# One kernel, one change: w_out made float32 during attention, kept in DRAM, and split in two parts at MoE 1

## The chip, the cores and the metric

The kernel runs on one core of one Trainium2 chip. The metric is the device time of one execution in microseconds. Five engines take part: PE (TensorE; its weight loads are listed as PEld), DVE (VectorE), ACT (ScalarE), POOL (GpSimd) and SP (SyncE, which only issues DMAs here). Each engine works through its own instructions in a fixed order and waits on semaphores for the others.

## The reference, cut to what matters

Three stages follow each other: attention with a position bias, a first MoE block (MoE 1, one dense "expert" with a SoLU and a layer norm), and a routed MoE with eight experts of which each token takes two. MoE 1 is the stage that reads `w_out`:

```
h    = x @ w_in                                # x 1152 x 512, w_in 512 x 1024
e    = exp(h - max(h));  sm = e / (sum(e) + 1e-9)
solu = h * sm
ln   = (solu - mean) / sqrt(var + 1e-6) * g_ln
out  = ln @ w_out                              # w_out 1024 x 512
```

`w_in` and `w_out` are float64 in DRAM. [...]

## The kernel before, in words

**Bias and attention.** The position bias is made in 18 pieces (`mix`, lines 192 to 210): eight threshold masks a piece (`masks`, line 179, spread over DVE, ACT and POOL by the MASK_ENG strings; 128 x 576 each), then matmuls (L202), then two DVE operations (L207, L208) into a tile that SP writes to DRAM (`biasd`, L210). Six pieces are made ahead of attention. Attention (loop at line 375) takes 40 units (5 row blocks x 4 head pairs x 2 batches) in 40 steps k, plus a tail. A step k holds, in this order: the transposes of unit k-2 (`tr`, L329 and L331, copied out by ACT at L332 and L334), at even k the product with v (`av`, L352, L361, then ACT L364 and DVE L365), the scores of unit k (`qk`: L301 on PE, L310 on DVE adds the bias and takes the row extreme, L317 on ACT is the exponential), and, for k below 24, half a bias piece (`bias_step`). Scores, bias matmuls and transposes share three PSUM banks named `d`; a matmul that writes a `d` bank waits until the reader of the bank three allocations earlier is done.

**The conversion.** `f64_parts` (line 244) turns a chunk of 128 x 512 float64 into float32 and its two parts in seven operations: ACT L251 (absolute value of the high word), a maximum (L252), DVE L254 (shift and mask), DVE L255 and L256 (`scalar_tensor_tensor`, which bring in the sign and the low word), ACT L257 (high part `hi`) and a subtraction L258 on POOL (low part `lo`). The first five work in a tile `t64`, of which there are TB = 2; the raw words lie in a tile `raw64`, of which there are RB64 = 3. L258 is the last to read a chunk's `t64`.

**w_in** (8 chunks) is converted inside the attention loop: from step 20 on a new chunk every second step (`CONV`), and each step runs one operation of every chunk in work. Every one of these is held by `keep_in_program_order`, so that it is issued behind everything that was written down before it for its engine. **w_out** (8 chunks) is fetched at the end of attention and converted in MoE 1 (`conv_out`, lines 429 to 434, called at lines 685 and 686 behind `stage1(1)`), all seven operations of a chunk one after the other; the maximum is on POOL for the first four chunks and on DVE for the rest. These are not held, so the scheduler places them by readiness.

**MoE 1** runs nine tiles of 128 tokens: `stage1` (line 439: split of x at L442 and L443, 24 matmuls L448 into one of two PSUM banks `ps`, then DVE L453, ACT L454, DVE L455 to L457, ACT L459, DVE L460; L457 is the last reader of the bank), `stage2a` (8 transposes L479, split at L401 and L402), `stage2` (24 matmuls L487 with the two parts of w_out) and `stage3` (L499, L504). `stage2(t)` stands in the code behind `stage1(t + 2)` and `stage2a(t + 1)`.

Of the kernel before, what the change touches and what calls it, by code (L numbers as in the profile page):

```python
# [9 lines left out]
F32 = mybir.dt.float32  # L10
F32R = mybir.dt.float32r
# [4 lines left out]
AF = mybir.ActivationFunctionType  # L16
OP = mybir.AluOpType
# [8 lines left out]
DM, FF, E = 512, 1024, 8  # L26
JB = 5
CAP = 320
W2B = 10
TB = 2  # L30
RB64 = 3
EB = 8
LAG = 2
# [7 lines left out]
AB = 1  # L41
SF = 3
TK = {0: (0, 1), 1: (2, 3)}
CONV = (20, 22, 24, 26, 28, 30, 32, 34)
TR = 7
FM = 2

# [16 lines left out]
def build(tc, I, O):  # L64
    nc = tc.nc
    ctx = ExitStack()
    with ctx:
        _build(tc, nc, ctx, I, O)


def _build(tc, nc, ctx, I, O):
    consts = ctx.enter_context(tc.tile_pool(name="consts", bufs=1, reuse_waits="tile"))

    dram = ctx.enter_context(tc.tile_pool(name="dram", bufs=1, space=bass.MemoryType.DRAM))
    x1d = dram.tile([NT * 128, DM], F32, name="x1d")
    biasd = dram.tile([NG, 128, S], F32, name="biasd")
    out = O["out"]

    nc.scalar.preload_act_table_set("natural_log_exp_and_others")
# [4 lines left out]
    V, P_ = nc.vector, nc.gpsimd  # L84
# [3 lines left out]
    def pool(stack, name, **kw):  # L88
        return stack.enter_context(tc.tile_pool(name=name, bufs=1, **{"reuse_waits": "tile", **kw}))
# [5 lines left out]
    cv = pool(ph_, "cv", side="right")  # L95
# [20 lines left out]
    def load_q(it):  # L116
        Q[it] = kvp.tile([128, 8, 128], F32, name="q", bufs=2)
        nc.sync.dma_start(Q[it], I["q5"][it])
# [27 lines left out]
    with tc.high_priority():  # L146
# [4 lines left out]
        for a in range(2):  # L151
            P_.tensor_tensor(out=W[:, a], in0=wab[:, a, None, :].to_broadcast([128, 4, H]),
                             in1=bd[:, 0:4, None].to_broadcast([128, 4, H]), op=OP.mult)
# [58 lines left out]
    def bias_step(s):  # L212

        m, gg = divmod(s, 2)
        if m >= NM:
            return
        if m + 1 < NM:
            masks(m + 1, 4 * gg, 4 * gg + 4)
        mix(m, gg)
# [3 lines left out]
    def bias_in(n):  # L223

        it, hp = divmod(n, 4)
        if it > 4:
            return
        r = 8 if it < 4 else 4
        src = biasd[8 * it:8 * it + r].rearrange("g (q h) j -> (g q) h j", h=H)[:, 2 * hp:2 * hp + 2]
        t = BT[it, hp] = btp.tile([128, 2, S], F32, name="bt", bufs=6)  # L230
        if it < 4:
            nc.sync.dma_start(t, src)
        else:
            for x in range(2):
                nc.sync.dma_start(t[64 * x:64 * x + 64, 0], src[:, x])


    def fetch(src):

        raw = cv.tile([128, 1024], F32, name="raw64", bufs=RB64)  # L240
        nc.sync.dma_start(raw.bitcast(mybir.dt.int64), src)
        return raw

    def f64_parts(raw, hi, lo, eng, eng2, pin=lambda i: i):

        tf = cv.tile([128, 512], F32, name="t64", bufs=TB)
        r = raw.bitcast(U32).rearrange("p (n two) -> p n two", two=2)
        w0, w1 = r[:, :, 0], r[:, :, 1]
        tu = tf.bitcast(U32)

        return (lambda: pin(nc.scalar.activation(tf, w1.bitcast(F32), AF.Abs)),  # L251
                lambda: pin(eng.tensor_scalar(tf, tf, 2.0 ** -15, None, op0=OP.max)),  # L252

                lambda: pin(V.tensor_scalar(tu, tu, 3, 0x3FFFFFF8, op0=OP.logical_shift_left, op1=OP.bitwise_and)),  # L254
                lambda: pin(V.scalar_tensor_tensor(tu, w1, 0xC0000000, tu, op0=OP.bitwise_and, op1=OP.bitwise_or)),  # L255
                lambda: pin(V.scalar_tensor_tensor(tu, w0, 29, tu, op0=OP.logical_shift_right, op1=OP.bitwise_or)),  # L256
                lambda: pin(nc.scalar.activation(hi, tf, AF.Copy)),  # L257
                lambda: pin(eng2.tensor_tensor(out=lo, in0=tf, in1=hi.bitcast(F32), op=OP.subtract)))  # L258

    CI = (V, P_)  # L260
    CO = [(P_, P_)] * 4 + [(V, P_)] * 4
    WI = {}

    def fetch_in(k, a):
        return fetch(I["w_in"][k * 128:k * 128 + 128, a * 512:a * 512 + 512])

    def conv_in(k, a, raw):

        if a == 0:
            if k < 3:  # L270
                t = bp.tile([128, 2304], F32R, name="mk", bufs=3)
                t = [t[:, 0:1024], t[:, 1024:2048]]
            else:
                t = [bp.tile([128, 1152], F32R, name="t", bufs=3) for w in range(2)]
            for n in range(2):
                WI[k, n] = [t[w][:, n * 512:n * 512 + 512] for w in range(2)]
        return f64_parts(raw, *WI[k, a], *CI, tc.keep_in_program_order)


    A = [(it, hp, b) for it in range(5) for hp in range(4) for b in range(B)]  # L280
# [39 lines left out]
    def tr(it, hp, b):  # L320

        u, es = SU[it, hp], ES.pop((it, hp, b))
        n = len(es)
        if b == 0:
            u.rest = psum.tile([128, 4, 128], F32, name="rest")
        pt = dbank().rearrange("p x (j i) -> p x j i", j=4)
        for x, e in enumerate(es):
            for jb in range(4):
                nc.tensor.transpose(pt[:, x, jb], e[:, jb * 128:jb * 128 + 128], ident)  # L329
        for x, e in enumerate(es):  # L330
            nc.tensor.transpose(u.rest[:, n * b + x], e[:, S - 128:S], ident)  # L331
        nc.scalar.activation(u.et[:, n * b:n * b + n, 0:4], pt[:, 0:n], AF.Copy)  # L332
        if b == 1:
            nc.scalar.activation(u.et[:, 0:2 * n, 4], u.rest[:, 0:2 * n], AF.Copy)  # L334
            u.rs = ap.tile([128, 4], F32, name="rs", bufs=3)
            V.tensor_scalar(u.rs[:, 0:2 * n], u.sums[:, 0:2 * n], 1e-9, None, op0=OP.add)
            V.reciprocal(u.rs[:, 0:2 * n], u.rs[:, 0:2 * n])
            if n == 2:
                u.rb = ap.tile([128, 4, 64], F32, name="rb", bufs=2)
                P_.tensor_copy(u.rb, u.rs[:, :, None].to_broadcast([128, 4, 64]))  # L340
# [29 lines left out]
    tc.keep_in_program_order(nc.scalar.preload_act_table_set("natural_log_exp_and_others"))  # L370
    bias_in(0)
    bias_in(1)
    chunks = [(k, a) for k in range(4) for a in range(2)]
    raws, conv = [], []
    for k in range(len(A) + LAG + 8):
        if k % 2 == 0 and k < len(A):
            bias_in(k // 2 + 2)
        if k % 8 == 6 and k // 8 + 1 < 5:
            load_q(k // 8 + 1)
        if LAG <= k < len(A) + LAG:  # L380
            tr(*A[k - LAG])
        if LAG <= k - 1 < len(A) + LAG and A[k - 1 - LAG][2] == 1:
            av(*A[k - 1 - LAG][:2])
        if k < len(A):
            qk(*A[k])
        bias_step(2 * PRE + k)
        if k == CONV[0] - 6:
            raws = [fetch_in(*chunks.pop(0)) for c in range(RB64)]
        if k in CONV:
            n = CONV.index(k)  # L390
            conv.append(list(conv_in(n // 2, n % 2, raws.pop(0))))
        for fs in conv:
            if fs:
                fs.pop(0)()
                if len(fs) == 2 and chunks:
                    raws.append(fetch_in(*chunks.pop(0)))
    pa.close()


# [16 lines left out]
    wop = pool(ph_, "wop", side="right")  # L416
    pm_ = ctx.enter_context(ExitStack())
    mp = pool(pm_, "mp", side="right")
    WO = {}

    def fetch_out(f):
        return fetch(I["w_out"][f * 128:f * 128 + 128, :])

    raws = [fetch_out(f) for f in range(RB64)]
    gB = mp.tile([128, FF], F32, name="gB")
    junk = mp.tile([128, FF], BF, name="junk")
    nc.sync.dma_start(gB, I["g_ln"].to_broadcast([128, FF]))

    def conv_out(f):
        WO[f] = [wop.tile([128, 512], F32R, name=f"wo{f}{w}") for w in range(2)]  # L430
        for g in f64_parts(raws.pop(0), *WO[f], *CO[f]):
            g()
        if f + RB64 < 8:
            raws.append(fetch_out(f + RB64))

    PASSES = ((0, 0), (0, 1), (1, 0))
    ST, SO = {}, {}
# [85 lines left out]
    def rt(shape, name, dt=F32, **kw):  # L523
        return mp.tile(shape, dt, name=name, **kw)
# [158 lines left out]
    nc.sync.dma_start(gw, I["gw"])  # L683
    stage1(1)
    for f in range(8):
        conv_out(f)
    noise = rt([128, NT, E], "noise")
    nc.sync.dma_start(noise, I["noise"])
    nc.sync.dma_start(cst, I["c_p"])
# [1 line left out]
    nc.sync.dma_start(iof, I["c_iota"].to_broadcast([128, NJ * 128]))  # L691
    trif = rt([128, 128], "trif")
    nc.sync.dma_start(trif, I["c_tri"])
    zero = mp.tile([128, DM // 2], F32, name="zero")
    tc.keep_in_program_order(nc.gpsimd.memset(zero, 0.0))
    for d in (0, DM // 2):
        nc.gpsimd.dma_start(out.rearrange("(t p) d -> p t d", p=128)[:, :, d:d + DM // 2],
# [98 lines left out]
    for e in range(E):  # L796
        W2 = [wload(w2s(e, f), ep, W2B, held=True) for f in range(4)] if e else []
        xt, w1 = XG.pop(e), W1.pop(e)
        for f in range(8):
            ph = psum.tile([128, 512], F32, name="phe", tag="h", bufs=3)  # L800
            for k in range(4):
                for n, (ww_, wx) in enumerate(PAS):
# [4 lines left out]
                                   op0=OP.max, op1=OP.subtract)  # L807
# [125 lines left out]
```

## Time and profile before

| | |
|---|---|
| median of 3 runs | 639.88 us (639.5 to 641.44) |
| the profiled execution | 640.86 us, its span 639.1 us |
| mean granted TensorE clock | 0.98 |
| busy in the span | PE 91%, PEld 74%, DVE 61%, ACT 53%, POOL 36% |
| chain that ended last | PE 65%, DVE 8%, POOL 7%, issue 7%, ACT 5%, DMA 4% |
| HBM | 67.66 MB read, 20.84 MB written |

The span is what the profiler saw; 1.8 us lie around it. Bias pieces ahead of attention fill the first 45 us or so, attention runs to about 230 us, MoE 1 from there to about 360 us, and the routed MoE to the end. A busy share is a mean over these stages. The chain of work that ended last is followed back from the last instruction, at each step to what released it.

### The profile page before, as it was taken

How to read it: one execution, taken by the hardware profiler on the slowest of the kernel's cores; microseconds unless marked ns; L12 is line 12 of the kernel's file. 1: busy time of each engine (PE TensorE's matmuls, PEld its weight loads, DVE VectorE, ACT ScalarE, POOL GpSimd, SP SyncE). 2: the span in 40 equal slices, each digit the busy share in tenths (PEclk: the TensorE clock that was granted, in tenths of full speed). 3: DMA queues.
4: the chain of work that ended last, by engine and by line, in shares of the span. 5: the costliest groups of instructions: out<-in, count | busy, mean ns of one | idle time of the engine just before them, and what ended most of it. 6: DMA issues, size and time to landing. Idle time of an engine off the chain costs nothing.

```text
span 639.1 us, 12762 instructions
## 1 busy us (share of the span) xinstructions
PE 581.8 (91%) x5068; PEld 475.4 (74%) x5068; DVE 392.2 (61%) x909; ACT 341.1 (53%) x657; POOL 231.9 (36%) x177
## 2 busy tenths in 40 slices
PE   0878999999999976999999989999999999999990
PEld 0556777777767754788888788888898989898980
DVE  4987777766665659765546788774647474543400
ACT  6935656565677645554436436554545454544410
POOL 4999998960111365410000302222222222222111
PEclk9979999999999997999999999999999999999996
DMA  8694415315421242140313235756565666636212
GB/s 318 263 340 140 156 75 186 110 48 214 161 85 67 71 149 98 40 158 18 125 53 92 96 119 170 249 144 212 163 199 182 182 194 162 222 66 191 35 18 29
DMA packets 33943, 89.44 MB, mean 140 GB/s; under 512 B 3600, under 2 KB 5136, under 8 KB 33872
## 3 DMA queue, kind: packets, MB, share of 16 engines
q1 hardware_dynamic: 26480, 72.04, 31.3%
q0 software_dynamic: 5808, 13.37, 10.5%
q10 hardware_dynamic: 1584, 3.11, 1.4%
q8 instruction: 42, 0.69, 0.4%
q14 instruction: 29, 0.24, 0.1%
HBM read 67.66 MB, written 20.84 MB: 138 GB/s over the span
## 4 chain that ended last, share of the span: by engine, by line
PE 65%; DVE 8%; POOL 7%; issue 7%; ACT 5%; DMA 4%; SPq 0%; POOLq 0%; DVEq 0%
PE phe L803 16%; PE poe L786 11%; PE ps L448 6%; PE d L301 4%; PE poe L790 4%; PE av L487 4%; POOL mk L190 4%; PE av L361 4%; PE d L202 3%; PE d L329 3%; DMA out<-y,si 3%; PE pt L487 3%; ACT e L317 2%; PE pg L674 1%; PE pt L504 1%
## 5 line engine op out<-in xcount | busy, mean ns | idle before, releaser
L190 POOL TENSOR_SCALAR mk<-T,thr 128x576 bf16<-128x576 f16 x67 | 116.1, 1746 | 12.7 <-PE d L202 8.7
L803 PE MATMUL phe<-xgt,wp 128*128 128x320 f32 x768 | 115.9, 310 | 2.3 <-ACT xgt L401 2.3
L803 PEld LDWEIGHTS phe<-xgt,wp 128*128 128x128 f32 x768 | 113.2, 188 | 3.0 <-ACT xgt L401 2.5
L637 POOL DMA_INDIRECT out<-y,si x24 | 39.4, 1642 | 149.2 <-ACT y L793 73.5
L786 PE MATMUL poe<-wp,hT 128*128 128x512 f32 x384 | 90.9, 393 | 0.0
L786 PEld LDWEIGHTS poe<-wp,hT 128*128 128x128 f32 x384 | 71.0, 188 | 14.2
L317 ACT ACTIVATE e<-e,nm 128x576 f32<-128x576 f32 x72 | 55.3, 769 | 42.4 <-DVE nm L310 42.4
L202 PE MATMUL d<-mk,wd 128*32 128x288 bf16 x1152 | 49.1, 304 | 21.8 <-POOL wd L169 14.3
L806 DVE SCALAR_TENSOR_TENSOR hT<-phe,hT 128x320 fp32r<-128x320 f32 x64 | 31.3, 490 | 50.2 <-ACT hT L805 49.7
L202 PEld LDWEIGHTS <-wd 128*32 128x32 f16 x1152 | 30.2, 101 | 42.5 <-issue 18.4
L310 DVE CUSTOM_DVE_ANT_0 e<-d,bt 128x576 f32<-128x576 f32 x72 | 51.9, 755 | 15.0 <-PE d L301 15.0
L448 PE MATMUL ps<-mk,xs 128*128 128x512 f32 x162 | 43.4, 418 | 8.3 <-DVE so L457 5.7
L402 DVE TENSOR_TENSOR wp<-w2raw,wp 128x1024 fp32r<-128x1024 f32 x32 | 39.1, 1225 | 18.4 <-ACT wp L401 16.7
L301 PE MATMUL d<-kv,q 64*128 64x288 f32 x256 | 48.9, 439 | 1.6 <-DVE t L208 1.3
L805 ACT ACTIVATE hT<-phe 128x320 fp32r<-128x320 f32 x64 | 28.0, 437 | 41.3 <-PE phe L803 41.3
L361 PE MATMUL av<-et,kv 128*64 128x128 f32 (+1 forms) x800 | 45.4, 265 | 0.0
L448 PEld LDWEIGHTS ps<-mk,xs 128*128 128x128 f32 x162 | 32.1, 201 | 16.9 <-ACT xs L442 7.1
L329 PE MATMUL d<-ident,e 128*128 128x128 f32 x288 | 40.5, 282 | 4.5 <-ACT et L332 2.6
L665 POOL DMA_INDIRECT xg<-x1d,gi x21 | 21.7, 1032 | 62.0 <-DVE si L627 46.0
L329 PEld LDWEIGHTS d<-ident,e 128*128 128x128 f32 x288 | 31.6, 142 | 16.7 <-DVE nm L310 6.9
L361 PEld LDWEIGHTS av<-et,kv 128*64 128x64 f32 x800 | 40.3, 137 | 3.6 <-issue 3.2
L332 ACT ACTIVATE et<-d 128x1024 f32<-128x1024 f32 (+1 forms) x40 | 37.2, 931 | 6.9 <-PE d L329 6.7
(194 smaller groups left out, 968.5 us busy)
## 6 DMA issues: line engine op xcount, KB each, us to landing
wraw<-moe_w SPq DMA_DIRECT2D x32, 512.0 KB, 5.3
w2raw<-moe_w SPq DMA_DIRECT2D x32, 512.0 KB, 6.5
biasd<-t SPq DMA_DIRECT2D x18, 576.0 KB, 3.4
bt<-biasd SPq DMA_DIRECT2D x16, 576.0 KB, 6.4
kv<-kv SPq DMA_DIRECT2D x8, 608.0 KB, 10.1
raw<-w_in SPq DMA_DIRECT2D x8, 512.0 KB, 5.1
raw<-w_out SPq DMA_DIRECT2D x8, 512.0 KB, 3.3
q<-q SPq DMA_DIRECT2D x5, 512.0 KB, 3.5
```

Source lines behind the costliest of these rows:

```text
L190: (V if e == "D" else P_).tensor_scalar(dst, w, thr[:, 0, q:q + 1], None, op0=OP.is_gt)
L202: nc.tensor.matmul(ps[32 * u:32 * u + 32, half, 0:288], WD[n][:, 32 * a:32 * a + 32], mk[:, 4 * gg + u, half * 288:half * 288 + 288], star ...
L301: nc.tensor.matmul(ss[x][:, a, 0:288], Q[it][h, n], k[h, a * 288:a * 288 + 288], start=True, stop=True)
L310: V.tensor_tensor_reduce(out=e.rearrange("p (a b) -> p a b", a=2), in0=ps[:, :, 0:288], in1=BT[it, hp][:, x].rearrange("p (a b) -> p a b", ...
L317: nc.scalar.activation(e, e, AF.Exp, bias=nm, scale=-1.0, accum_out=u.sums[:, c + x:c + x + 1])
L329: nc.tensor.transpose(pt[:, x, jb], e[:, jb * 128:jb * 128 + 128], ident)
L361: nc.tensor.matmul(o[64 * x:64 * x + 64, 0, b, 0:n], v[:, jb, 64 * x:64 * x + 64], w, start=(jb == 0), stop=(jb == JB - 1))
L448: nc.tensor.matmul(ph[:, a], xs[wx][:, k], WI[k, a][ww], start=(k == 0 and n == 0), stop=(k == 3 and n == 2))
L487: nc.tensor.matmul(po, lt[wx][:, f], WO[f][ww], start=(f == 0 and n == 0), stop=(f == 7 and n == 2))
L637: nc.gpsimd.indirect_dma_start(out=dst, out_offset=bass.IndirectOffsetOnAxis(ap=si, axis=0), in_=y, in_offset=None, compute_op=OP.add, bou ...
L786: nc.tensor.matmul(po, hT[f][wh][:, j:j + R], W2[f // 2][ww_][:, c:c + N], start=(f == 0 and m == 0), stop=(f == 7 and m == 2))
L803: nc.tensor.matmul(ph[:, 0:CAP], w1[k][ww_][:, f * 128:f * 128 + 128], xt[wx][:, k], start=(k == 0 and n == 0), stop=(k == 3 and n == 2))
```

## The change

`f64_parts` is split. `f32` holds the first five operations (the maximum always on DVE). The parts are two operations more, ACT and POOL. The attention loop now converts 16 chunks: the eight of w_out from step 4 on and the eight of w_in from step 20 on as before, again one operation a step and chunk. A chunk of w_out ends with a DMA on SP's queue that writes the float32 tile to a DRAM buffer `w32d`. At MoE 1, `parts_out` reads a chunk back into a `t64` tile and makes the two parts. TB goes from 2 to 3, the raw fetches are now held in program order (the first three at step 1), and the zeros for the output are written from a `t64` tile instead of a tile of their own.

```diff
-TB = 2
+TB = 3
-CONV = (20, 22, 24, 26, 28, 30, 32, 34)
+CONV = (4, 6, 8, 10, 12, 14, 16, 18, 20, 22, 24, 26, 28, 30, 32, 34)
...
+    w32d = dram.tile([8, 128, 512], F32, name="w32d")
...
+    def words(c):
...
+        raw = cv.tile([128, 1024], F32, name="raw64", bufs=RB64)
+        tc.keep_in_program_order(nc.sync.dma_start(raw.bitcast(mybir.dt.int64), src))
...
+    def conv_out(c, raw):
+        t = t64()
+        return f32(raw, t) + [lambda: tc.keep_in_program_order(nc.sync.dma_start(w32d[c], t))]
...
-        if k == CONV[0] - 6:
-            raws = [fetch_in(*chunks.pop(0)) for c in range(RB64)]
+        if k == CONV[0] - 3:
+            raws = [words(chunks.pop(0)) for c in range(RB64)]
         if k in CONV:
             n = CONV.index(k)
-            conv.append(list(conv_in(n // 2, n % 2, raws.pop(0))))
+            conv.append([5] + (conv_out(n, raws.pop(0)) if n < 8 else conv_in(*divmod(n - 8, 2), raws.pop(0))))
...
-    raws = [fetch_out(f) for f in range(RB64)]
...
-    def conv_out(f):
-        WO[f] = [wop.tile([128, 512], F32R, name=f"wo{f}{w}") for w in range(2)]
-        for g in f64_parts(raws.pop(0), *WO[f], *CO[f]):
-            g()
-        if f + RB64 < 8:
-            raws.append(fetch_out(f + RB64))
+    def parts_out(f):
+        hi, lo = WO[f] = [wop.tile([128, 512], F32R, name=f"wo{f}{w}") for w in range(2)]
+        t = t64()
+        nc.sync.dma_start(t, w32d[f])
+        nc.scalar.activation(hi, t, AF.Copy)
+        P_.tensor_tensor(out=lo, in0=t, in1=hi.bitcast(F32), op=OP.subtract)
...
     for f in range(8):
-        conv_out(f)
+        parts_out(f)
...
-    zero = mp.tile([128, DM // 2], F32, name="zero")
+    zero = t64()[:, 0:DM // 2]
```

## Rows read from the trace of the kernel before

**Rows 1.** Windows: start and end, length, busy PE, PEld, DVE, ACT, POOL, clock, DMA
```profile
78.20:88.80 10.60, 10.34 (x144) 7.83 (x143) 7.84 (x19) 6.20 (x14) 9.02 (x7) 1.00 0.26 97
232.00:264.00 32.00, 24.69 (x101) 19.41 (x102) 25.99 (x46) 15.90 (x31) 17.46 (x13) 0.89 0.22 74
```

**Rows 2.** Chain of waits in MoE 1: start, length, engine, line, count
```profile
286.23 2.10 PE av L487 x9
...
293.17 5.60 PE ps L448 x24
298.77 0.87 PE pt L479 x8
299.64 2.10 PE pt L487 x9
```

**Rows 3.** Timeline, MoE 1's front: start, length, engine, work, idle before it and releaser
```profile
230.38 1.19 PE L448 MATMUL ps<-mk,xs 128*128 128x512 f32 x4 [0.89 <-ACT xs L442]
...
233.25 3.54 PE L448 MATMUL ps<-mk,xs 128*128 128x512 f32 x14 [1.68 <-DVE xs L443]
...
248.06 1.27 DVE L457 SCALAR_TENSOR_TENSOR so<-ps,st,so 128x1024 f32<-128x1024 f32 x1
...
249.49 7.20 PE L448 MATMUL ps<-mk,xs 128*128 128x512 f32 x18 [5.70 <-DVE so L457]
```

**Rows 4.** Groups of the conversion's operations: busy us, mean ns, idle before and releasers
```profile
L251 ACT ACTIVATE t<-raw 128x512 f32<-128x512 f32 x16 | 10.7, 670 | 11.4 <-POOL mk L258 5.4 <-POOL wo L258 4.8 <-POOL t L258 1.2
L252 DVE TENSOR_SCALAR t<-t 128x512 f32<-128x512 f32 x12 | 5.4, 451 | 13.4 <-ACT t L251 13.4
L254 DVE TENSOR_SCALAR t<-t 128x512 uint32<-128x512 uint32 x16 | 9.4, 590 | 8.0 <-POOL t L252 8.0
L255 DVE SCALAR_TENSOR_TENSOR t<-raw,t 128x512 uint32<-128x512 uint32 x16 | 11.0, 685 | 0.1
L256 DVE SCALAR_TENSOR_TENSOR t<-raw,t 128x512 uint32<-128x512 uint32 x16 | 12.1, 756 | 0.1
```

**Rows 5.** Timeline of two attention steps that still hold bias work
```profile
81.74 0.42 DVE L365 TENSOR_TENSOR XA<-XA,av 128x256 f32<-128x256 f32 x1 [1.41 <-ACT XA L364]
...
85.11 1.02 ACT L332 ACTIVATE et<-d 128x1024 f32<-128x1024 f32 x1 [0.20 <-PE d L329]
...
86.50 0.76 DVE L310 CUSTOM_DVE_ANT_0 e<-d,bt 128x576 f32<-128x576 f32 x1 [0.93 <-PE d L301]
...
87.99 0.86 PEld L329 LDWEIGHTS d<-ident,e 128*128 128x128 f32 x8 [0.31 <-DVE nm L310]
```

**Rows 6.** Timeline: DVE operations that ran beside POOL operations
```profile
77.59 6.96 POOL L190 TENSOR_SCALAR mk<-T,thr 128x576 bf16<-128x576 f16 x4 [0.79 <-PE d L202]
...
233.12 1.77 DVE L256 SCALAR_TENSOR_TENSOR t<-raw,t 128x512 uint32<-128x512 uint32 x1
...
236.89 2.94 POOL L252 TENSOR_SCALAR t<-t 128x512 f32<-128x512 f32 x2
...
238.41 0.83 DVE L254 TENSOR_SCALAR t<-t 128x512 uint32<-128x512 uint32 x1 [3.52 <-POOL t L252]
```

**Rows 7.** Timeline of attention after the last bias piece, and of its end
```profile
163.50 2.40 PE L361 MATMUL av<-et,kv 128*64 128x128 f32 x40
...
171.95 2.40 PE L361 MATMUL av<-et,kv 128*64 128x128 f32 x40
...
174.75 0.67 ACT L251 ACTIVATE t<-raw 128x512 f32<-128x512 f32 x1 [0.89 <-POOL mk L258]
...
180.97 2.40 PE L361 MATMUL av<-et,kv 128*64 128x128 f32 x40
...
224.17 0.43 DVE L254 TENSOR_SCALAR t<-t 128x512 uint32<-128x512 uint32 x1 [1.78 <-POOL t L252]
```

**Rows 8.** DMA issues: tile, queue, count, KB each, median us to landing
```profile
biasd<-t SPq DMA_DIRECT2D x18, 576.0 KB, 3.4
...
raw<-w_out SPq DMA_DIRECT2D x8, 512.0 KB, 3.3
```

More of the change, by code (lines that the diff above doesn't have):

```diff
@@ L235, in bias_in, with f32 @@
                 nc.sync.dma_start(t[64 * x:64 * x + 64, 0], src[:, x])
[L238 to L246, printed above, removed]
+    def f32(raw, tf):
+        pin = tc.keep_in_program_order
         r = raw.bitcast(U32).rearrange("p (n two) -> p n two", two=2)
@@ L249, in f64_parts, with t64 @@
         tu = tf.bitcast(U32)
-        return (lambda: pin(nc.scalar.activation(tf, w1.bitcast(F32), AF.Abs)),
-                lambda: pin(eng.tensor_scalar(tf, tf, 2.0 ** -15, None, op0=OP.max)),
+        return [lambda: pin(nc.scalar.activation(tf, w1.bitcast(F32), AF.Abs)),
+                lambda: pin(V.tensor_scalar(tf, tf, 2.0 ** -15, None, op0=OP.max)),
                 lambda: pin(V.tensor_scalar(tu, tu, 3, 0x3FFFFFF8, op0=OP.logical_shift_left, op1=OP.bitwise_and)),
                 lambda: pin(V.scalar_tensor_tensor(tu, w1, 0xC0000000, tu, op0=OP.bitwise_and, op1=OP.bitwise_or)),
[L256 to L261, printed above, removed]
+                lambda: pin(V.scalar_tensor_tensor(tu, w0, 29, tu, op0=OP.logical_shift_right, op1=OP.bitwise_or))]
+    def t64():
+        return cv.tile([128, 512], F32, name="t64", bufs=TB)
+    def words(c):
+        k, a = divmod(c - 8, 2)
+        src = I["w_out"][c * 128:c * 128 + 128, :] if c < 8 else I["w_in"][k * 128:k * 128 + 128, a * 512:a * 512 + 512]
+        raw = cv.tile([128, 1024], F32, name="raw64", bufs=RB64)
+        tc.keep_in_program_order(nc.sync.dma_start(raw.bitcast(mybir.dt.int64), src))
+        return raw
     WI = {}
-    def fetch_in(k, a):
-        return fetch(I["w_in"][k * 128:k * 128 + 128, a * 512:a * 512 + 512])
+    def conv_out(c, raw):
+        t = t64()
+        return f32(raw, t) + [lambda: tc.keep_in_program_order(nc.sync.dma_start(w32d[c], t))]
     def conv_in(k, a, raw):
@@ L276, in conv_in @@
                 WI[k, n] = [t[w][:, n * 512:n * 512 + 512] for w in range(2)]
-        return f64_parts(raw, *WI[k, a], *CI, tc.keep_in_program_order)
+        t, (hi, lo), pin = t64(), WI[k, a], tc.keep_in_program_order
+        return f32(raw, t) + [lambda: pin(nc.scalar.activation(hi, t, AF.Copy)),
+                              lambda: pin(P_.tensor_tensor(out=lo, in0=t, in1=hi.bitcast(F32), op=OP.subtract))]
     A = [(it, hp, b) for it in range(5) for hp in range(4) for b in range(B)]
@@ L372, in _build @@
     bias_in(1)
-    chunks = [(k, a) for k in range(4) for a in range(2)]
+    chunks = list(range(16))
     raws, conv = [], []
@@ L386, in _build @@
         bias_step(2 * PRE + k)
-        if k == CONV[0] - 6:
-            raws = [fetch_in(*chunks.pop(0)) for c in range(RB64)]
+        if k == CONV[0] - 3:
+            raws = [words(chunks.pop(0)) for c in range(RB64)]
         if k in CONV:
             n = CONV.index(k)
-            conv.append(list(conv_in(n // 2, n % 2, raws.pop(0))))
+            conv.append([5] + (conv_out(n, raws.pop(0)) if n < 8 else conv_in(*divmod(n - 8, 2), raws.pop(0))))
         for fs in conv:
[L393 to L396, printed above, removed]
+            if len(fs) > 1:
+                fs.pop(1)()
+                fs[0] -= 1
+                if fs[0] == 0 and chunks:
+                    raws.append(words(chunks.pop(0)))
     pa.close()
@@ L419, in _build @@
     WO = {}
-    def fetch_out(f):
-        return fetch(I["w_out"][f * 128:f * 128 + 128, :])
-    raws = [fetch_out(f) for f in range(RB64)]
     gB = mp.tile([128, FF], F32, name="gB")
```

## The prediction, made blind

> **What bounds the kernel now.** I read the windows first, stage by stage, since the busy shares of the whole span mix stages. In attention with bias work, two steps take 10.6 us and PE is busy for 10.34 of them; DVE for 7.84, ACT for 6.20, POOL for 9.02 [rows 1]. So PE ends these steps, with little room on DVE and POOL. In the front of MoE 1 it is the reverse: of 32 us PE is busy for 24.69 and DVE for 25.99, and the granted clock falls to 0.89 on average [rows 1]. The chain of waits then shows MoE 1 in its steady state, where one tile takes 299.64 - 286.23 = 13.41 us and all pieces are PE's [rows 2]. The timeline of the front says why it is slower: the first matmuls stop for 1.68 us because the DVE split of x is late, and the third tile's matmuls wait 5.70 us for L457, the last reader of their bank, which DVE reaches only at 248.06 because the conversion of w_out stands in the same queue. [...]
>
> **What goes: conversion work in MoE 1's front.** Per chunk one ACT operation (0.67), the maximum, L254, L255 and L256: for eight chunks 8 x (0.45 + 0.59 + 0.69 + 0.76) = 20 us of DVE at the groups' means (four maxima were on POOL, so 18) and 5.4 us of ACT [rows 4]. The price on the path is taken from PE, not from this sum. From the first L448 (230.38) to the start of the third tile's stage2 (286.23) pass 55.85 us [rows 2, 3]. At full clock PE has there five stage1 (5 x 5.60), four stage2a (4 x 0.87) and two tiles of stage2 with stage3 (13.41 - 5.60 - 0.87 = 6.94 each): 28.0 + 3.5 + 13.9 = 45.4 us [rows 2]. So 10.4 us at most can come back. Not all will: the first transposes need the whole chain of the first tile (L453 to L460), about 1.4 us behind the end of the second tile's stage1 if PE keeps the order of the code, and some 0.5 us go to the first split of x. I take 8.5, between 3 (ACT or the reloads late instead, below) and 10.4. What stays per chunk, one ACT copy and one POOL subtraction, is off the path as long as the eighth chunk is ready by the first stage2, some 18 us after the start (three stage1 and two stage2a). The reload of 256 KB should land no later than the 512 KB fetch did (3.3) [rows 8], and three `t64` tiles are in rotation, so I count under 2 us a chunk: ready after about 16.
>
> **What goes: the wait for `t64`.** With two tiles the ACT operation of a chunk waits for the POOL subtraction of the chunk two before (5.4 us in all for POOL mk, 0.89 of it at 174.75), and what ACT does next, the copy of the scores' product, is late with it [rows 4, 7]. Two steps without that wait took 171.95 - 163.50 = 8.45 us, the next two with it 180.97 - 171.95 = 9.02 [rows 7]. With three tiles the chunk before last is long done. I take 0.5 us for each of four pairs after the bias, 0.4 for each of the four short pairs of the last row block, and at the end, where DVE stood 1.78 us behind POOL's maximum of a w_out chunk [rows 7], 0.5 of that: together 4.0 us, bounds 1 and 6.
>
> **What is added: w_out's five operations beside the bias.** About eight pairs of steps (k = 4 to 23, less the ramp at both ends) get one chunk each: on ACT 0.67 (on top of 6.20 of 10.6, in idle time), on DVE two `tensor_scalar` and two `scalar_tensor_tensor`, 0.42 + 0.42 + 0.69 + 0.69 without neighbours, which is 2.2 on top of 7.84, so DVE comes to 10.0 of 10.6 [rows 1, 4]. A sum below the period isn't enough, as DVE works in order. In the even step the operations fall behind L208, where DVE was idle for 0.93 us until PE had the next scores, and PE in turn waited 0.31 us for that L310 [rows 5]: L310 is on the path. One of each kind, 1.04 us net of overlap, goes into 0.93: 0.1 us late. In the odd step the idle stretch, before L365, is 1.41 us and takes it [rows 5]. Both kinds run beside POOL masks now, where the trace has hardly a case. The lower bound is no stretch at all. The nearest row is L254 beside a POOL `tensor_scalar`, 0.83 instead of 0.42; the far row is L256 beside a POOL subtraction, 1.77 instead of 0.69 [rows 6]. With half of the nearest row's stretch (0.2 to 0.3, since not every operation meets one) the even step is 0.35 late: 8 x 0.35 = 2.8 us. Bounds: below nothing (-0.5) isn't excluded, since a shift of DVE can also let a POOL mask through earlier, and 12 at the top, with 1.5 us a pair.
>
> [...]
>
> **The other added pieces at nothing.** SP issues eight more fetches and eight writes: in the two steps of rows 1 the DMA share is 0.26, and 512 + 256 KB a pair are little more than one bias write and one bias load. Behind a fetch that waits for its raw tile stand bias writes and loads on SP; the loads lead their use by several steps. The write to DRAM now holds the `t64` tile until it has landed: it is queued right behind the bias write (3.4 us to landing [rows 8]), with about half a pair, 5.3 us, until the ACT operation that reuses the tile. If that cover is gone, ACT stands, and L332 behind it, which at 85.11 had 0.2 us of idle time before it [rows 5]. [...] The zero tile costs nothing.
>
> **The sum.** 640.86 (the profiled execution, span 639.1) - 8.5 - 4.0 + 2.8 = 631.2 us. The median shown is 1.0 below that execution, so I say 630.2.
>
> **The rivals.**
> - *Slower: DVE becomes the bound beside the bias.* If each of the four operations is stretched by about 0.55 us (half of what L256 lost), the even step is 1.04 + 1.1 - 0.93 = 1.2 late and the odd one 1.04 + 1.1 - 1.4 = 0.75, together 1.95 a pair, 15.6 in all: 640 - 12.5 + 15.6 = 643. It takes the whole gain from 12.5 / 8 = 1.56 us a pair on, and is slower beyond the uncertainty from 1.8. For it: 85% of POOL's time is taken there, mostly by masks of 1.74 us each [rows 1, 6], and DVE already has 7.84 of 10.6. Against it: L255 has a mean of 0.685 over all 16, one of them beside a POOL maximum [rows 4], so a one-input POOL operation need not stretch it. Chance 0.11.
> - *The front stays late for another reason.* The reloads wait for the POOL subtractions, and ACT, which takes its copies in order, stands in front of the exponentials; then the front gives back 3 instead of 8.5: 635.7. For it: ACT waited there 4.8 us for POOL [rows 4]; against it, no DVE link is left in the chunk's chain. Chance 0.14.
> - *The DRAM write holds `t64` too long.* 1 us a pair of ACT standing, eight pairs: 638.2. Against it the 5.3 us of cover. Chance 0.07.
> - [...] Chance 0.03, as the trace has one-input operations that were not shut out.
>
> The forecast has 0.65. The range: best 640 - 10.4 - 6 + 0 = 623.5, and up to the third rival and a little beyond, 639.5, which leaves the slower rivals outside. Below 0.3% (1.9 us) a measurement of this kernel can't be told from no change. Faster: the forecast, most of the second rival, half of the third, 0.80; same 0.09; slower, most of the first rival and the last, 0.11.
>
> **What would show it.** Right: no PE wait over 2 us in MoE 1's first 20 us and the clock at its upper level there; the distance from the first L448 to the third stage2 near 47 us; no ACT wait for POOL at the abs operation in attention, pairs of 8.4 us after the bias; pairs of 10.8 to 11 us with bias work, with PE waiting longer for L310. Wrong: bias pairs above 12 us with DVE busy throughout, L255 and L256 above 1.2 us beside masks, ACT waiting for a DMA in attention, or stage2(0) waiting for w_out's parts.

## The result, and the profile after

The changed kernel takes 632.5 us (median of 4 runs, 631.38 to 633.24), the kernel before 640.01 beside it: ratio 0.9872, 95% interval 0.9858 to 0.9886, so 7.5 us less. The forecast was 630.2 with a range of 623.5 to 639.5. Direction and mechanism held; the gain is three quarters of the forecast one.

The page of the profile after (span 630.9 us) shows first that TensorE's work is the same (581.8 us busy before) and only its idle time has shrunk. In the clock's row, a digit for each fortieth of the span, the dip in MoE 1's front is gone (before: the 7 in the sixteenth slice); a small new one, in slice 24, is taken up in run 7. The last row here is the one of the page before:

```profile
PE 581.1 (92%) x5068; PEld 475.8 (75%) x5068; DVE 392.2 (62%) x913; ACT 339.7 (54%) x657; POOL 229.3 (36%) x173
...
PEclk9989999999999999999999989999999999999997
...
PEclk9979999999999997999999999999999999999996
```

A window over MoE 1's front answers to the second of [rows 1], and two windows show a pair of bias steps with w_out's operations in them, the first beside POOL's masks, the second after the last mask (columns as there):

```profile
232.00:264.00 32.00, 30.43 (x142) 24.12 (x141) 17.86 (x39) 17.85 (x36) 18.16 (x16) 1.00 0.44 142
...
100.50:111.63 11.13, 10.47 (x143) 7.81 (x142) 10.21 (x23) 6.63 (x14) 9.88 (x7) 1.00 0.82 285
...
145.00:155.60 10.60, 10.34 (x144) 7.82 (x143) 8.53 (x20) 6.65 (x14) 0.40 (x1) 1.00 0.78 281
```

In the front PE is busy for 30.43 of 32 us instead of 24.69, DVE for 17.86 instead of 25.99, and the granted clock is 1.00 instead of 0.89. Beside the masks DVE is busy for 10.21 us of a pair, which now takes 11.13 instead of 10.58; without masks on POOL, at 145 us, the pair is back at 10.6 although w_out's and w_in's chunks are both in work there.

Cut at the same instructions in both traces (DVE's score operation of a step, the first L448, the first matmul of the third stage2, the first and last matmul of the experts), the spans compare so:

| stretch | before | after | difference | forecast |
|---|---|---|---|---|
| start to step 4 | 61.32 | 60.56 | -0.8 | 0 |
| step 4 to step 24 | 105.79 | 109.22 | +3.4 | +2.8 |
| step 24 to step 39 | 57.41 | 54.52 | -2.9 | -4.0 |
| step 39 to MoE 1's first matmul | 5.87 | 5.96 | +0.1 | 0 |
| from there to the third tile's stage2 | 55.61 | 46.30 | -9.3 | -8.5 |
| from there to the first expert | 92.91 | 92.71 | -0.2 | 0 |
| first matmul to last first-layer matmul of the experts | 230.84 | 232.20 | +1.4 | 0 |
| to the end | 29.33 | 29.42 | +0.1 | 0 |

The differences add up to -8.2 us, as the two spans do (639.1 and 630.9).

The timeline of the front answers to [rows 3] (start, length, engine, work, idle before it and releaser):

```profile
230.27 4.47 PE L452 MATMUL ps<-mk,xs 128*128 128x512 f32 x18 [0.89 <-ACT xs L446]
...
236.03 0.63 ACT L437 ACTIVATE wo<-t 128x512 fp32r<-128x512 f32 x1 [3.13 <-DMA t<-w32d]
...
239.35 0.63 ACT L437 ACTIVATE wo<-t 128x512 fp32r<-128x512 f32 x1 [1.27 <-DMA t<-w32d]
239.89 1.10 ACT L458 ACTIVATE so<-ps,st 128x1024 f32<-128x1024 f32 x1
...
242.93 3.04 PE L452 MATMUL ps<-mk,xs 128*128 128x512 f32 x12 [1.19 <-DVE so L461]
...
276.57 1.64 PE L491 MATMUL av<-wo,lt 128*128 128x512 f32 x6
```

The first stage1 no longer stops for the split of x, and the third waits 1.19 us for its bank instead of 5.70. That rest is not DVE's: ACT takes its copies of the reloaded chunks in order, stands 3.13 and 1.27 us for reloads, and so starts the first tile's exponential only at 239.89. It is the mechanism of the second rival, at about a fifth of the price named there.

The timeline of an even bias step, and of the odd one behind it, answers to [rows 5]:

```profile
106.77 1.72 POOL L192 TENSOR_SCALAR mk<-T,thr 128x576 bf16<-128x576 f16 x1
107.12 0.93 DVE L252 SCALAR_TENSOR_TENSOR t<-raw,t 128x512 uint32<-128x512 uint32 x1
...
107.98 0.79 DVE L250 TENSOR_SCALAR t<-t 128x512 uint32<-128x512 uint32 x1
...
108.69 0.74 DVE L317 CUSTOM_DVE_ANT_0 e<-d,bt 128x576 f32<-128x576 f32 x1
...
109.49 0.67 PE L204 MATMUL d<-mk,wd 128*32 128x288 bf16 x16 [0.40 <-DVE nm L317]
...
110.28 4.24 POOL L192 TENSOR_SCALAR mk<-T,thr 128x576 bf16<-128x576 f16 x2 [1.25 <-PE d L204]
...
111.83 0.67 DVE L251 SCALAR_TENSOR_TENSOR t<-raw,t 128x512 uint32<-128x512 uint32 x1
112.43 0.41 DVE L248 TENSOR_SCALAR t<-t 128x512 f32<-128x512 f32 x1
```

The idle stretch of 0.93 us before the score operation is gone: two conversion operations take 1.57 us there, PE waits for the score operation behind them, and the pair of steps is 0.55 us longer. Both are stretched (0.68 and 0.42 us where POOL has no masks), while the mask beside them keeps its 1.72 us. In the odd step it is the other way round: the two operations at 111.83 and 112.43 keep their length, and of the two masks in 4.24 us the second, beside them, takes 2.5 us instead of 1.72.

### The profile page after: what moved, and what is told of

It is laid out like the page before. It is cut to its first block, busy times and chain, and to the rows that moved or that the text cites. A ratio compares the mean times of both kernels' runs of the same rounds, so it can differ in the third digit from the quotient of the medians.

```text
span 630.9 us, 12806 instructions
## 1 busy us (share of the span) xinstructions
PE 581.1 (92%) x5068; PEld 475.8 (75%) x5068; DVE 392.2 (62%) x913; ACT 339.7 (54%) x657; POOL 229.3 (36%) x173
## 5 line engine op out<-in xcount | busy, mean ns | idle before, releaser
L192 POOL TENSOR_SCALAR mk<-T,thr 128x576 bf16<-128x576 f16 x67 | 119.7, 1805 | 10.7 <-PE d L204 7.2
L807 PE MATMUL phe<-xgt,wp 128*128 128x320 f32 x768 | 117.3, 312 | 2.3 <-ACT xgt L409 2.3
L807 PEld LDWEIGHTS phe<-xgt,wp 128*128 128x128 f32 x768 | 114.6, 190 | 3.0 <-ACT xgt L409 2.5
L368 PE MATMUL av<-et,kv 128*64 128x128 f32 (+1 forms) x800 | 47.3, 266 | 0.0
L452 PE MATMUL ps<-mk,xs 128*128 128x512 f32 x162 | 39.7, 397 | 2.1 <-DVE so L461 1.2
L409 ACT ACTIVATE wp<-w2raw 128x1024 fp32r<-128x1024 f32 x32 | 34.0, 1061 | 13.1 <-DMA w2raw<-moe_w 6.4
```

Of the source, the lines that this page charges most:

```text
L192: (V if e == "D" else P_).tensor_scalar(dst, w, thr[:, 0, q:q + 1], None, op0=OP.is_gt)
L368: nc.tensor.matmul(o[64 * x:64 * x + 64, 0, b, 0:n], v[:, jb, 64 * x:64 * x + 64], w, start=(jb == 0), stop=(jb == JB - 1))
L452: nc.tensor.matmul(ph[:, a], xs[wx][:, k], WI[k, a][ww], start=(k == 0 and n == 0), stop=(k == 3 and n == 2))
L807: nc.tensor.matmul(ph[:, 0:CAP], w1[k][ww_][:, f * 128:f * 128 + 128], xt[wx][:, k], start=(k == 0 and n == 0), stop=(k == 3 and n == 2))
```

## The experiments

**1. The third tile alone.** The kernel before with TB = 3, and nothing moved.

```diff
-TB = 2
+TB = 3
...
-    zero = mp.tile([128, DM // 2], F32, name="zero")
+    zero = cv.tile([128, 512], F32, name="t64", bufs=TB)[:, 0:DM // 2]
```

> The kernel before with three t64 tiles, and nothing else of the change. Theory A (the wait for t64 cost attention its end): steps 24 to 39 and the step to MoE 1 take 2 to 3 us less, as between the two kernels (57.4 us before, 54.5 after, from the score operations of step 24 to those of step 39), the run is at about 637 to 638 us. Theory B (the end was faster because no w_out chunk is in work there): steps 24 to 39 stay within 0.7 us of before, the run at 639.5 to 640.

Measured: 640.4 us, ratio 0.9998 (0.9985 to 1.0011). Steps 24 to 32 take 35.17 us instead of 35.83, steps 32 to 39 the same 21.6. The waits of ACT over steps 24 to 32 say why the lost wait bought so little (who waited for whom: us in total, times, longest). Before:

```profile
ACT e L317 <- DVE nm L310: 6.5, 5, 1.6
ACT t L251 <- POOL mk L258: 3.3, 4, 0.9
ACT XA L364 <- PE av L361: 1.7, 1, 1.7
```

With three tiles:

```profile
ACT e L317 <- DVE nm L310: 7.9, 5, 1.6
ACT XA L364 <- PE av L361: 2.9, 5, 1.7
```

The 3.3 us for POOL are gone, and 2.6 of them came back as waits for DVE and PE: pairs of 8.79 us are set by the loop of scores, exponential and transposes. Theory B holds for the run's time. That this loop sets the pair is read from these waits; no run changes the loop itself. (MoE 1's first matmul came 1.4 us earlier in this profile; its experts took 232.55 us instead of 230.84, on which more below.)

**2. MoE 1's front without the DVE work.** The kernel before, w_out's chunks reduced in MoE 1.

```diff
-        for g in f64_parts(raws.pop(0), *WO[f], *CO[f]):
-            g()
+        g = f64_parts(raws.pop(0), *WO[f], *CO[f])
+        for i in (0, 5, 6):
+            g[i]()
```

> The kernel before, but the four operations of a w_out chunk between its absolute value and its high part are left out in MoE 1 (the parts are made of other numbers); fetches, the ACT operations and the POOL subtraction stay. Theory A (the DVE queue made MoE 1's front late): from the first matmul of stage1 to the third tile's stage2 46 to 48 us as in the changed kernel (46.3; before 55.6), the clock at its upper level there, the run at about 631 us. Theory B (the fetches, or ACT and POOL): still 52 us or more.

Measured: 633.5 us in one run, 2.5 above the expected 631: its experts take 232.98 us instead of 230.84 (run 7 says more on that), and the end behind them 0.7 us more. The granted clock is 1.00 over the front (231 to 263 us). PE's timeline:

```profile
228.98 4.46 PE L449 MATMUL ps<-mk,xs 128*128 128x512 f32 x18 [0.89 <-ACT xs L443]
...
241.97 3.04 PE L449 MATMUL ps<-mk,xs 128*128 128x512 f32 x12 [1.53 <-DVE so L458]
...
275.95 2.33 PE L488 MATMUL av<-wo,lt 128*128 128x512 f32 x9
```

From the first to the last of these rows 46.97 us, as in the changed kernel and not as before, with all eight fetches, sixteen ACT operations and the POOL subtractions still in place. So the front was late for the conversion operations left out (three on DVE, the maximum on DVE or POOL); what the fetches and ACT's operations still cost lies within the 1.53 us that the third stage1 waits here. The run also shows what the end of attention gained: steps 32 to 39 take 19.56 us here with two tiles, and 19.37 in the changed kernel, against 21.58 before. It was w_out's first chunks, converted there among the last scores, and not the `t64` wait.

**3. The bias steps without w_out's DVE operations.** The changed kernel.

```diff
-        return f32(raw, t) + [lambda: tc.keep_in_program_order(nc.sync.dma_start(w32d[c], t))]
+        ops = f32(raw, t)
+        return ops[:1] + [lambda: None] * 4 + [lambda: tc.keep_in_program_order(nc.sync.dma_start(w32d[c], t))]
```

> The changed kernel, but of w_out's chunks beside the bias the four DVE operations are left out; fetch, the ACT operation and the write to DRAM stay. Theory A (DVE's queue costs the 0.55 to 0.6 us a pair of steps beside masks): pairs of 10.58 us from step 8 to 20 instead of 11.13 to 11.2, the run at about 629 us. Theory B (ACT's operation, SP's queue or the extra DMA): pairs stay at 11.0 or more.

Measured: pairs of 10.58 us from step 8 to 20 (one of 10.66), so the 0.55 us a pair are DVE's. A window over one pair:

```profile
100.00:110.58 10.58, 10.32 (x154) 7.81 (x142) 7.83 (x19) 6.64 (x14) 9.01 (x6) 1.00 0.64 231
```

DVE is at 7.83 as before, ACT with the added operation at 6.64. The run as a whole missed its figure: 635.95 us instead of 629. Two single pairs were long, the one up to step 4 (16.27 us) and the one from step 22 (15.19); runs 7 and 8 show long pairs at the same two places in other profiles.

**4. POOL's masks replaced by a constant.** The changed kernel.

```diff
+            elif e == "P" and m > PRE + 1:
+                P_.memset(dst, 1.0)
```

> The changed kernel, but from the eighth bias piece on POOL writes a constant in place of its masks (these parts of the bias are left out); DVE and ACT make theirs as before, and w_out's operations stay. Theory A (POOL masks stretch w_out's DVE operations beside them): L252 and L250 of w_out go back from 0.93 and 0.79 us to 0.68 and 0.42, pairs of 10.6 us from step 10 to 20. Theory B (DVE simply holds too much work): the operations may shorten, but pairs stay at 11.0 or more.

Measured: pairs of 10.58 us with all of w_out's operations in place; 629.75 us in one run. Window and timeline:

```profile
100.00:110.58 10.58, 10.32 (x146) 7.81 (x144) 9.67 (x23) 6.62 (x14) 3.21 (x8) 1.00 0.82 297
...
106.28 0.68 DVE L254 SCALAR_TENSOR_TENSOR t<-raw,t 128x512 uint32<-128x512 uint32 x1
106.88 0.42 DVE L252 TENSOR_SCALAR t<-t 128x512 uint32<-128x512 uint32 x1
107.29 0.76 DVE L319 CUSTOM_DVE_ANT_0 e<-d,bt 128x576 f32<-128x576 f32 x1
...
108.86 2.81 POOL L192 MEMSET mk<- 128x576 bf16 x5 [6.53 <-PE d L206]
...
110.75 0.68 DVE L253 SCALAR_TENSOR_TENSOR t<-raw,t 128x512 uint32<-128x512 uint32 x1
111.35 0.59 DVE L250 TENSOR_SCALAR t<-t 128x512 f32<-128x512 f32 x1
```

The same two operations (their lines are 254 and 252 here) take 1.01 us together and the score operation follows at once. DVE is still busy for 9.67 us of the pair, so its load as a whole isn't the cause: it is the stretch beside POOL's masks, in the one place where nothing covers it. Theory A. The run takes POOL's work away from the even step altogether (the five memsets of a pair stand beside the odd step's operations), so it doesn't tell a mask from a shorter POOL operation there; run 5, with all masks in place, adds what is missing.

**5. The operations spread by the idle stretches.** The changed kernel, with the maximum and the shift both in the odd step, so that an even step holds one operation.

```diff
-        return f32(raw, t) + [lambda: tc.keep_in_program_order(nc.sync.dma_start(w32d[c], t))]
+        ops = f32(raw, t)
+        return ops[:1] + [lambda: (ops[1](), ops[2]())] + ops[3:] + [lambda: tc.keep_in_program_order(nc.sync.dma_start(w32d[c], t))]
...
-            conv.append([5] + (conv_out(n, raws.pop(0)) if n < 8 else ...
+            conv.append([4 if n < 8 else 5] + (conv_out(n, raws.pop(0)) if n < 8 else ...
```

> The changed kernel with w_out's DVE operations spread by where DVE has time: the maximum and the shift both in the odd step, so that the even step holds one scalar_tensor_tensor (0.69 to 0.93 us in an idle stretch of 0.93) and the odd one three operations. Theory A (only what falls into the even step beyond its idle stretch counts): pairs of 10.6 to 10.7 us, the run 3 us below the changed kernel, about 629.5. Theory B (DVE as a whole, or its sharing with POOL, sets the pair): pairs at 11.0 or more, the run as the changed kernel.

Measured: 629.48 us (628.13 to 629.92), ratio to the kernel before 0.9822 (0.9793 to 0.9851). Steps 4 to 24 take 106.06 us: pairs of 10.58, one of 10.87. DVE's timeline over an even and an odd step:

```profile
96.05 1.04 DVE L251 SCALAR_TENSOR_TENSOR t<-raw,t 128x512 uint32<-128x512 uint32 x1
97.05 0.76 DVE L318 CUSTOM_DVE_ANT_0 e<-d,bt 128x576 f32<-128x576 f32 x1
...
100.21 0.68 DVE L252 SCALAR_TENSOR_TENSOR t<-raw,t 128x512 uint32<-128x512 uint32 x1
100.81 0.41 DVE L248 TENSOR_SCALAR t<-t 128x512 f32<-128x512 f32 x1
...
101.96 0.41 DVE L250 TENSOR_SCALAR t<-t 128x512 uint32<-128x512 uint32 x1
```

The one operation of the even step is stretched to 1.04 and just fits; three in the odd step keep their length and cost nothing. The same amount of DVE work, otherwise placed, takes back 3.2 us. A second measurement, five rounds beside the changed kernel on one chip:

> The spread version (e4), five rounds: 3.2 us below the changed kernel by the bias steps (106.06 instead of 109.22 us from step 4 to 24), so about 629.3. If the first measurement was a lucky one, within 1 us of the changed kernel.

> The changed kernel, five rounds, beside the spread version on the same chip: about 632.4, with single runs from 631.2 to 633.3. If the half clock at the routed MoE's start (1.5 us) comes and goes by the execution, the profile may or may not have it.

Measured: 2.35 us between the two instead of 3.2, and a wider spread of single runs than expected: 630.5 (628.34 to 633.38) against 632.85 us (630.91 to 636.93), the ratios to the kernel before are 0.9831 (0.9808 to 0.9854) and 0.9866 (0.9842 to 0.9889). Their intervals overlap a little; with those of the first measurements (0.9822 and 0.9872) the spread version is the fastest of the three kernels, by 2 to 3 us.

**6. Two tiles in the changed kernel, and w_in spread too.**

```diff
-TB = 3
+TB = 2
```

> The changed kernel with two t64 tiles instead of three. Theory A (the write to DRAM and the POOL subtraction hold t64 for less than two chunks' time only because there are three): ACT waits for w32d's write beside the bias, pairs above 11.2 us, and for POOL after it, pairs of 8.9; the reloads of w_out at MoE 1 come later; the run 2 to 10 us above the changed kernel. Theory B (the third tile does nothing): the same as the changed kernel, 632.5.

Measured: 648.44 us in one run, worse than both theories' figures. ACT's waits over steps 6 to 24:

```profile
ACT t L247 <- DMA w32d<-t: 15.1, 7, 4.9
```

The tile is held until its write has landed, and ACT stands 15.1 us in seven places for it; pairs go up to 16.88 us. The third tile buys nothing in the old order (run 1) and the new order needs it: without it the run is slower than the kernel before.

> The kernel with spread operations (e4), and w_in's chunks spread in the same way, so that each is done a step earlier. Theory A (after the bias DVE is off the path: pairs of 8.79 us are set by ACT and PE): within 0.7 us of e4, about 629.5. Theory B (DVE's order still costs there): pairs below 8.6 us after step 24, 1 us or more below e4.

With w_in's operations grouped as well the run takes 629.85 us (628.95 to 630.47), as expected by theory A; pairs after step 24 are 8.93 instead of 8.79.

**7. What comes and goes between executions.** Three profiles of the changed kernel are alike to 0.1 us in MoE 1's front (46.30, 46.36, 46.30) and in the pairs of steps 8 to 18 (but for one of 11.44 us instead of 11.13 in the third), but their spans are 630.9, 629.9 and 635.1.

> The changed kernel once more, for a second profile. Theory A (the 3.4 us at half clock at the start of the routed MoE, and with it 232.2 instead of 230.8 us for its experts, come and go between executions of one kernel): it may be absent, with experts at 230.7. Theory B (they belong to the change): they are there again at the same place. Steps 8 to 20 11.1 to 11.2 us a pair and 46.3 us for MoE 1's front either way.

> The kernel before once more, for a second profile. Its steps to be the same to 0.1 us (105.8 us from step 4 to 24, 55.6 for MoE 1's front); if the half clock at the routed MoE's start is a matter of the execution and not of the change, it may show here, with experts at 232.2 instead of 230.8 us.

The window over the start of the experts and PE's first matmuls there, first in the first profile after, then in the second one:

```profile
366.00:396.00 30.00, 27.74 (x218) 24.76 (x218) 22.75 (x50) 15.68 (x32) 5.98 (x4) 0.94 0.57 197
...
369.29 3.98 PE L807 MATMUL phe<-xgt,wp 128*128 128x320 f32 x16 [2.26 <-ACT xgt L409]
```

```profile
366.50:396.50 30.00, 27.73 (x229) 24.60 (x228) 24.44 (x58) 16.66 (x35) 5.99 (x4) 1.00 0.61 209
...
369.83 3.46 PE L807 MATMUL phe<-xgt,wp 128*128 128x320 f32 x22 [2.27 <-ACT xgt L409]
```

In the first, the granted clock is 0.50 for 3.4 us (369.0 to 372.4), from near the end of a wait of 2.26 us in which PE stood for ACT. The second has the same wait, 2.27 us, and a granted clock of 1.00 over its whole window. The experts take 232.20 us there and 230.65 in the second. So the +1.4 us of the table come and go with the execution, theory A. Both profiles of the kernel before were without it (230.84 and 230.65), of the changed kernel's three two had it, of the spread version's two one; run 1, the old order with a third tile, had it too (232.55). Whether the new timing makes it likelier can't be told from so few.

In the third profile, of 635.1 us, the pair from step 22 takes 13.70 us instead of 10.58. SP's issue of the write, the ACT operation behind it, PE, and a window over PE's next 5 us:

```profile
157.07 0.47 SPq L270 DMA_DIRECT2D w32d<-t  x1
...
164.55 0.67 ACT L247 ACTIVATE t<-raw 128x512 f32<-128x512 f32 x1 [2.02 <-DMA w32d<-t]
...
166.18 2.11 PE L204 MATMUL d<-mk,wd 128*32 128x288 bf16 x32 [1.70 <-ACT et L339]
...
165.00:170.00 5.00, 3.82 (x44) 2.99 (x43) 3.03 (x6) 3.19 (x8) 0.00 (x0) 0.66 0.56 206
```

This write took 7.5 us to land, behind bias loads, a fetch and a bias write that kept the DMA engines near full (a share of 0.95 from 156 to 160 us); the page of the first profile has a median of 4.5 for the eight writes:

```profile
w32d<-t SPq DMA_DIRECT2D x8, 256.0 KB, 4.5
```

ACT stood 2.0 us for it and PE 1.7 for ACT, and the clock then fell, to 0.66 over the window; together they can account for the 3.1 us. It is the third rival, once in a while instead of in each pair. Run 3's pair from step 22 has the same mark: a write that took 8.8 us to land, and ACT standing 3.4 us for it.

**8. A stall ahead of step 4.** In the five-round profile of the spread version (span 631.5) the pair up to step 4 takes 17.12 us instead of 11.79 in the first one. POOL and PE there, and last a piece of the chain of waits of the kernel before:

```profile
43.21 13.89 POOL L192 TENSOR_SCALAR mk<-T,thr 128x576 bf16<-128x576 f16 x8
...
57.05 0.39 POOL L348 COPY rb<-rs 128x256 f32<-128x256 f32 x1
...
57.49 0.69 PE L360 MATMUL av<-ident,rb 128*128 128x128 f32 x2 [3.84 <-POOL rb L348]
58.11 4.54 PE L369 MATMUL av<-et,kv 128*64 128x128 f32 x40
...
46.52 8.33 POOL mk L190 x5
```

A POOL copy that PE needs stands behind eight masks. The steps before came earlier than usual (the first score operation at 38.56 us instead of 39.64), PE waited the longer, and the 40 matmuls behind the wait took 4.54 us, where 40 take 2.40 in [rows 7]. POOL's masks are in the chain of waits of this stretch in the kernel before as well, and of the change only SP's first three fetches stand there.

## Why the prediction was right, step by step

**The front of MoE 1: right.** DVE's queue was the cause (run 2). 46.3 us against a forecast of "near 47": -9.3 instead of -8.5. (By the same matmul in both traces the distance before is 55.61 us; the forecast's 55.85 ends at a later piece of the chain.) The wait that I allowed for the transposes of the first tile was smaller, since PE took half of the third stage1 first; ACT's wait for reloads cost 1.2 instead. The granted clock is 1.00 over the front's window, as expected; before, it was 0.50 from 249.5 to 255.5 us, at the matmuls behind the wait of 5.70 us [rows 3].

**The operations beside the bias: right in mechanism and place, a little small.** The even step is late, the odd one is not; 0.55 to 0.6 us a pair instead of 0.35, so pairs of 11.13 to 11.20 us, a little above the 10.8 to 11 that were named as the sign. The stretch per operation was put at half of the nearest row's; in the even step it came out as 0.25 to 0.33 us for the `scalar_tensor_tensor` and 0.37 for the `tensor_scalar`, which is nearly all of the 0.41 of that row [rows 6]. In the odd step there was none; POOL's mask beside the operations took 2.5 us instead of 1.72. That only six of the eight pairs paid it (the last two run after POOL's masks) kept the term at 3.4.

**The wait for `t64`: wrong.** The step said 3.6 us for the eight pairs and 0.5 for w_out's maximum on POOL (4.1 as written, entered as 4.0). Measured is 0.7 for the wait (run 1) and 2.0 to 2.2 for w_out's operations at attention's end (runs 1 and 2). The error was to compare one pair of 8.45 us without a wait, directly behind the last bias piece, with 9.02 [rows 7]: the steady pair without any such wait is 8.79, as the next wait, ACT for DVE's row extremes, stands just behind. And w_out's operations there were costed by the one wait that named them, while their DVE time in the middle of the short steps of the last row block cost four times as much. That 2.9 of the 4.0 us came all the same is luck: most of it was earned by the other cause.

**The pieces at nothing: right in most executions.** SP, the fetches and ACT's operation cost nothing in steady state (run 3: pairs of 10.58 us with them in place). The write's hold on the tile has less cover than I thought: I took the bias write's 3.4 us for its landing; the median came out as 4.5, and with 7.5 us it reaches the path (run 7). The traffic was judged too lightly as well. One bias write and one bias load a pair, of 576 KB each, are 1152 KB, so the added 768 KB are two thirds of them and not "little more", and the DMA share of 0.26 is that of a quiet pair. Two pairs earlier the same trace has 0.76:

```profile
57.00:67.60 10.60, 10.00 (x139) 7.49 (x140) 6.90 (x16) 4.92 (x10) 10.60 (x8) 1.00 0.76 278
```

**What the forecast had no term for:** -0.8 us ahead of step 4 and +1.4 in the experts. The second comes and goes with the clock (0.94 and 1.00 over the experts' first 30 us in two profiles of the changed kernel, run 7); the first isn't settled, as that stretch varies from 60.6 to 61.1 us over the changed kernel's profiles and was 61.3 in both of the kernel before.

**The rivals.** The slower one, DVE as the bound beside the bias, had its place right and its price wrong: 0.55 us a pair, where it needed 1.56 to eat the gain. The last rival, with its chance of 0.03, did not come: the cost beside the bias was 3.4 us in all. The DVE operation at 107.12, beside a mask that began at 106.77 and ran to 108.49, ended at 108.05 and not behind the mask: it took 0.25 us more than without one. The mask beside the odd step's operations takes 2.5 us instead of 1.72, longer by about what they have left to run when it starts (0.84 us, from 112.0 to 112.84). Why the two directions differ, no run here shows.

## What to carry to other kernels

Idle time of an engine isn't all of one kind. Work moved into it was free here where it fitted into one idle stretch with its real length, and it cost time where it ran over a stretch that the critical path passes through. So count the operations against each stretch, and put them into the long one: the same four DVE operations cost 0.55 us a pair of steps in one order and nothing in the other. A wait that the trace shows may be worth only the distance to the next wait behind it: 3.3 us of waits removed left the time as it was (run 1), so try it alone. Where a buffer comes free by a DMA's landing instead of an engine's operation, give it one more buffer than the order of the code needs: with two `t64` tiles ACT stood 15.1 us for the writes and the run took 648.44 us, with three 632.5 (run 6).

## What the runs showed of the hardware that was not expected

A POOL `tensor_scalar` of 128 x 576 takes 1.72 us, and who pays when DVE works beside it depends on the place. In the even steps DVE's `scalar_tensor_tensor` and `tensor_scalar` took 0.25 to 0.37 us longer beside it; in the odd steps, where DVE had begun before the mask, they kept their 0.67 and 0.41 us and the mask took 2.5. Beside a POOL memset of the same tile the `scalar_tensor_tensor` kept its 0.68 us, while the maximum, a `tensor_scalar`, took 0.59 instead of 0.42 (run 4). A wait of PE of 2.3 us ahead of the experts was followed by 3.4 us at a granted clock of 0.50 in the first profile of the changed kernel and by none in the second, where the clock was 1.00 and the experts took 1.55 us less (run 7).
